# Attention and two feed-forward layers on one core: VectorE turns keys and queries, with smaller PSUM tiles and a new order of units

## The chip, the cores and the metric

The kernel runs on one core of a Trainium2 chip. The metric is the device time of one execution in microseconds (us). TensorE is called PE, VectorE DVE, ScalarE ACT, GpSimd POOL, and SyncE, which issues every DMA here, SP.

## The reference, cut to what matters

All in float32: 4 batches of 8 heads, 576 positions, 64 columns a head; then two feed-forward layers on 2304 tokens of 512 columns, with 2048 hidden columns.

```python
scores = (q @ k.T) / sqrt(64)                # per batch and head
scores = where(block_i >= block_j, scores, -1e9)   # blocks of 64 positions
attn = exp(scores - max); attn = attn / (attn.sum + 1e-9)
x = attn @ v                                 # heads side by side: 2304 x 512
x = g1(x @ w_in1) @ w_out1                   # g1: squared ramp between -1 and 1
x = (h * cos(h)) @ w_out2,  h = x @ w_in2
```

Scores need the 64 columns of a head on the partitions for both operands, so keys and queries have to be turned (positions by columns becomes columns by positions) before PE can multiply them.

## The kernel before, in words

Two heads make a pair: 16 pairs, n = 0 to 15. For each pair, `load` (L430) brings K and Q from memory as 96 partitions x 6 groups of positions, two DMAs each (one a head, 576 runs of 256 bytes). `prep` (L464) turns one of them: six PE transposes (L472) into a PSUM tile, then one copy of 128x576 to SBUF by ACT or DVE (`cp`, recorded at L185 on ACT, L189 and L190 on DVE; the copy of Q carries the scale). There are 32 preps, named "pk" (keys) and "pq" (queries). The unit's end issues the load for pair n + 2 into the buffer that it has read.

`scores` (L482) is a unit "S3", "S2" or "S0": score matmuls (L495) into a tile of two PSUM banks, maxima by DVE (L504), exponentials with row sums by ACT (L510), then `recip` (an addition, L519, and a reciprocal, L523, both DVE) and `div`, in which POOL scales P (L532). `tails` ("tl", L553) does the last 64 positions of two pairs together. `trans` ("T3", "T2", "T0", "Ta", "Tb") transposes P on PE (L590) and copies it to SBUF; `pv` ("PV", L618), `pv_halves` ("PX", L629), `pv_tails` ("Pt", L673) and `tail_halves` ("Px") multiply by V; the result goes through the tile xs to memory. P has one buffer.

PSUM has eight banks, held as four tiles of two banks. `ps_take` picks the tile that a model says is free first, or one that the unit names. A wait is for the whole tile, both banks.

`PERIOD` (L1161) is the order of units on PE for two pairs; it is laid out for all pairs in turn, with pair 1's preps put in by hand at the start. Behind the last scores and tails, the remaining units alternate with the first hidden products of layer 1 (`mm1`, L755). The opening runs idle matmuls (L702) on zeros while the first loads come.

All of this is given to `Plan` (L27), which simulates the engines P, V, A, G and S (SP) with a cost for each piece and emits every engine's instructions in simulated order. The order of units on PE is fixed by `PERIOD`; where a copy may run on two engines ("AV": ACT or DVE) the plan chooses, and it sets SP's order of DMAs too. During the pairs, 14 of the 32 weight blocks of layer 1 (512 KB each) are loaded and split (L260, L265, L277, L286, L292, L187, L181), one behind each "S3". Layer 1 then runs PE back to back (L755, L796), and layer 2 follows (L938, L1030).

Of the kernel before, what the change touches and what calls it, by code (L numbers as in the profile page):

```python
# [102 lines left out]
def attn_moe_moe_kernel(ctx: ExitStack, tc: tile.TileContext, q, k, v, w_in1, w_out1, w_in2, w_out2, out):  # L103
# [259 lines left out]
    BANKS = [0.0] * 4  # L363
    tiles, pt = {}, [0.0]

    def ps_take(cost, hold, allowed=range(4)):
        i = min(allowed, key=lambda i: (BANKS[i], i))
        start = max(pt[0], BANKS[i])
        pt[0] = start + cost
        BANKS[i] = pt[0] + hold  # L370
        n = len(tiles)
        tiles[n] = None
        return n, i, ("ps", i)

    def ps_of(n, i):
        if tiles[n] is None:
            tiles[n] = M.ps[i // 2].tile([128, 2, 512], F32, name=f"t{i}", tag=f"t{i}")
        return tiles[n]
# [6 lines left out]
    def attention_buffers(stack):  # L385
# [4 lines left out]
        M.R = [[sb.tile([TK, S // TK, 2, D], F32, name=f"r{nm}{c}") for c in range(2)] for nm in "kq"]  # L390
        M.xs = [sb.tile([128, S], F32, name=f"xs{c}") for c in range(3)]
        M.sm = sb.tile([128, 3, 3, 10], F32, name="sm")

# [20 lines left out]
    def probs(i):  # L414
        return M.A2.view(256 * P_BLOCK[i], [S if i in ("a", "b") else 64 * i + 64])
# [14 lines left out]
    def load(n, which):  # L430
# [23 lines left out]
        else:  # L454
            t = M.R[which][n % 2]
            keys = [("raw", which, n % 2)]

            def emit():
                for h in range(2):
                    nc.sync.dma_start(out=t[:, :, h, :], in_=src[b, 2 * p + h].rearrange("(t p) d -> p t d", p=TK))  # L460

        dma(294 + 64 * (which == 2), [], keys, emit)

    def prep(n, which, allowed=range(4)):  # L464
        nt = S // TK // 2
        t = M.R[which][n % 2]
        r, i, key = ps_take(0.5, 1.2, allowed)

        def emit():
            ps = ps_of(r, i)  # L470
            for j in range(2 * nt):
                pin(nc.tensor.transpose(  # L472
                    ps[:, j // nt, (j % nt) * TK:(j % nt + 1) * TK], t[:, j].rearrange("p h d -> p (h d)"),
                    ident[0:TK, 0:TK],
                ))

        tensor(0.5, [("raw", which, n % 2)], [key], emit)
        dst = (M.K, M.Q)[which][n % 2]
        cp("AV", S, lambda: dst.rearrange("p (a b) -> p a b", a=2), lambda: ps_of(r, i)[:, :, 0:HALF],
           [key], [("KQ"[which], n % 2)], scale=(1.0, scale)[which])  # L480

    def scores(n, u, allowed=range(4)):  # L482
# [3 lines left out]
        r, i_, key = ps_take(SCORES[u], {3: 3.4, 2: 3.6, 0: 3.4}[u], allowed)  # L486

        def emit():
            ps = ps_of(r, i_)
            Q, K = M.Q[c], M.K[c]  # L490
            for i, a, off in subs:
                for h in range(2):
# [3 lines left out]
                        out=ps[o:o + 64, a, off:off + 64 * i + 64], lhsT=Q[hd, 64 * i:64 * i + 64],  # L496
# [3 lines left out]
        tensor(SCORES[u], [("K", c), ("Q", c)], [key], emit)  # L500
        for i, a, off in subs:
            nk = 64 * i + 64
            do("V", 0.065 + nk / 960.0, [key], sk(0, n, i, i + 1), lambda e, i=i, a=a, off=off, nk=nk: pin(
                nc.vector.tensor_reduce(  # L504
                    out=stat(0, n, i, i + 1), in_=ps_of(r, i_)[:, a, off:off + nk], axis=AX.X, op=ALU.max, negate=True,
                )))
        for i, a, off in subs:
            nk = 64 * i + 64
            do("A", 0.24 + 0.00083 * nk, [key] + sk(0, n, subs[-1][0], subs[0][0] + 1), [("P", i)] + sk(1, n, i, i + 1),
               lambda e, i=i, a=a, off=off, nk=nk: pin(nc.scalar.activation(  # L510
                   out=probs(i)[:, 0:nk], in_=ps_of(r, i_)[:, a, off:off + nk], func=ACTF.Exp,
                   bias=stat(0, n, i, i + 1), accum_out=stat(1, n, i, i + 1),
               )))
        recip(n, subs[-1][0], subs[0][0] + 1)
        for i, a, off in subs:
            div(n, i, i)
# [9 lines left out]
    def div(n, e0, i):  # L526

        nk = S if i in ("a", "b") else 64 * i + 64
        main = nk - 64 if i in HALF_IN else nk

        def piece(out, w, writes):
            do("G", 0.25 + 0.00082 * w, sk(2, n, e0, e0 + 1) + [("P", i)], [writes], lambda e: pin(nc.gpsimd.tensor_scalar(  # L532
                out=out(), in0=probs(i)[:, 0:main] if w == main else probs(i)[:, main:nk],
# [3 lines left out]
        piece(lambda: probs(i)[:, 0:main], main, ("P", i))  # L537
        if i in HALF_IN:
            piece(lambda: M.A2.view(256 * HALF_OF[HALF_IN[i]], [64]), 64, ("PH", i))

    def tails(n, allowed=range(4)):

        both = [ps_take(0.5, 2.6 + 0.8 * x, allowed[x:][:1] if len(allowed) == 2 else allowed) for x in range(2)]

        def emit():
            ps = [ps_of(r, i) for r, i, _ in both]
            for a in range(2):
                for x in range(2):
                    for h in range(2):
# [4 lines left out]
                            out=ps[x][o:o + 64, a, 0:HALF], lhsT=M.Q[m % 2][hd, S - TAIL:S],  # L554
# [618 lines left out]
    def part_one():  # L1173
# [59 lines left out]
        for x in seq[:last + 1]:  # L1233
            unit(*x)
# [96 lines left out]
```

## Time and profile before

| | us |
|---|---|
| median of 3 runs | 928.95 (928.42 to 933.76) |
| the profiled execution's own time | 928.82 |
| its span in the trace | 927.0 |
| PE busy | 914.4 |
| DVE, ACT, POOL busy | 655.9, 562.2, 171.5 |
| the pairs' stage, from the first matmul to the first product of layer 1 that stands behind attention's last | 0.99 to 179.76 |

Busy means that an instruction of the engine is under way; a busy PE may still work below its best rate. Time outside the span (1.8 us) is the start and end of the program. Granted clock is TensorE's clock as a share of its full speed. A pass of `PERIOD` is called a period below; from 57.82 to 137.04 us four of them stand in the trace, cut where the eight transposes of a "T3" begin.

### The profile page before, as it was taken

To read this page: it belongs to the slowest core of one execution; us is meant where nothing else is said; L and a number is where in the kernel's file an instruction comes from. 1 tells how busy PE (TensorE), PEld (TensorE's weight loads), DVE (VectorE), ACT (ScalarE), POOL (GpSimd) and SP (SyncE) were. 2 spreads that over 40 slices of the span, in tenths; PEclk is the share of its full clock that TensorE was granted. 3 is DMA by queue.
4 is the path that set the end of the run, shared out by engine and by line. 5 is a ranking of instruction groups with operands and counts; after the bars stand their busy time and mean duration, and the time that the engine had idled before them with its cause. 6 is when DMAs were issued, how large, how long until landed. Compare 5 with 4: busy or idle time off the path is not lost.

```text
span 927.0 us, 18120 instructions
## 1 busy us (share of the span) xinstructions
PE 914.4 (99%) x6916; PEld 819.0 (88%) x6916; DVE 655.9 (71%) x1044; ACT 562.2 (61%) x1015; POOL 171.5 (19%) x289
## 2 busy tenths in 40 slices
PE   8999999999999999999999999999999999999998
PEld 6777777788888889988888889999999999999997
DVE  5899888768666666676226323999959899388883
ACT  5897878788666656556335434676416674166641
POOL 2667776542101112231000000000000000000000
PEclk9999999999999999999999999999999999999999
DMA  9876674584866666755120506877898878877781
GB/s 190 196 193 178 173 177 111 181 268 140 288 213 215 238 197 231 237 199 205 45 91 23 204 23 227 250 254 245 274 343 256 263 241 260 296 254 251 247 263 54
DMA packets 145670, 189.93 MB, mean 205 GB/s; under 512 B 70320, under 2 KB 103600, under 8 KB 145584
## 3 DMA queue, kind: packets, MB, share of 16 engines
q1 hardware_dynamic: 145584, 188.78, 64.6%
q8 instruction: 55, 0.90, 0.4%
q14 instruction: 31, 0.25, 0.1%
HBM read 145.23 MB, written 43.52 MB: 204 GB/s over the span
## 4 chain that ended last, share of the span: by engine, by line
PE 94%; DVE 2%; ACT 2%; POOL 1%; issue 1%; DVEq 0%; ACTq 0%; POOLq 0%
PE a L796 21%; PE h L755 21%; PE q L1030 20%; PE q L938 19%; PE t L590 4%; PE t L495 3%; PE t L618 3%; PE t L472 1%; ACT n L510 1%; DVE sm L504 1%; PE t L629 1%; PE t L702 1%; PE t L553 1%; POOL n L532 1%; PE t L673 0%
## 5 line engine op out<-in xcount | busy, mean ns | idle before, releaser
L938 PE MATMUL q<-m 128*128 128x384 f32 x1008 | 175.2, 334 | 0.0
L938 PEld LDWEIGHTS q<-m 128*128 128x128 f32 x1008 | 174.7, 188 | 0.1
L1030 PE MATMUL q<-m,n 128*128 128x256 f32 x1260 | 153.8, 283 | 0.0
L1030 PEld LDWEIGHTS q<-m,n 128*128 128x128 f32 x1260 | 152.4, 192 | 0.0
L796 PE MATMUL a<-g,m 128*128 128x512 f32 (+1 forms) x540 | 118.3, 368 | 0.6 <-DVE xs L190 0.6
L768 ACT ACTIVATE f<-h,half 128x512 f32<-128x512 f32 (+1 forms) x80 | 51.5, 644 | 103.7 <-PE h L755 103.6
L770 DVE SCALAR_TENSOR_TENSOR f<-f,h 128x512 f32<-128x512 f32 (+1 forms) x80 | 50.5, 632 | 88.9 <-ACT f L769 88.3
L796 PEld LDWEIGHTS a<-g,m 128*128 128x128 f32 x540 | 94.6, 189 | 17.5 <-ACT f L769 0.7
L532 POOL TENSOR_SCALAR n<-n,sm 128x64 f32<-128x64 f32 (+6 forms) x184 | 85.9, 488 | 44.1 <-DVE sm L523 30.2
L181 DVE TENSOR_TENSOR g<-f,g 128x512 fp32r<-128x512 f32 (+1 forms) x80 | 54.3, 679 | 37.2 <-ACT g L185 31.8
L510 ACT ACTIVATE n<-t,sm 128x384 f32<-128x384 f32 (+7 forms) x128 | 62.2, 510 | 9.1 <-DVE sm L504 4.9
L755 PE MATMUL h<-m 128*128 128x512 f32 (+1 forms) x324 | 67.5, 356 | 0.0
L755 PEld LDWEIGHTS h<-m 128*128 128x128 f32 x324 | 53.9, 189 | 8.4
L504 DVE TENSOR_REDUCE sm<-t 128x1 f32<-128x256 f32 (+7 forms) x128 | 50.0, 448 | 15.7 <-PE t L495 15.5
L185 ACT ACTIVATE g<-f 128x512 fp32r<-128x512 f32 (+1 forms) x69 | 40.4, 586 | 33.8 <-DVE f L770 33.8
L292 DVE SCALAR_TENSOR_TENSOR f<-f 128x512 uint32<-128x512 uint32 x64 | 44.7, 706 | 20.1 <-ACT f L277 17.1
L907 ACT ACTIVATE f<-f,hpi 128x768 f32<-128x768 f32 x48 | 44.6, 929 | 16.3 <-DVE f L903 16.3
L796 PE MATMUL a<-g,n 128*128 128x512 f32 (+1 forms) x240 | 52.5, 368 | 0.0
L590 PE MATMUL t<-ident,n 128*128 128x128 f32 x360 | 49.0, 277 | 3.4 <-ACT xs L185 0.9
L755 PE MATMUL h<-x,m 128*128 128x512 f32 x216 | 52.0, 389 | 0.0
L796 PEld LDWEIGHTS a<-g,n 128*128 128x128 f32 x240 | 42.1, 189 | 7.5
L769 ACT ACTIVATE f<-f 128x512 f32<-128x512 f32 (+1 forms) x80 | 46.9, 587 | 1.8
(134 smaller groups left out, 1565.3 us busy)
## 6 DMA issues: line engine op xcount, KB each, us to landing
m<-w2i SPq DMA_DIRECT2D x84, 512.0 KB, 4.4
m<-w2o SPq DMA_DIRECT2D x84, 512.0 KB, 4.2
f<-in_moe_w_in_dram SPq DMA_DIRECT2D x32, 512.0 KB, 4.5
f<-in_moe_w_out_dram SPq DMA_DIRECT2D x32, 512.0 KB, 4.4
w2i<-f SPq DMA_DIRECT2D x8, 1024.0 KB, 4.9
w2o<-f SPq DMA_DIRECT2D x8, 1024.0 KB, 4.2
w2i<-o SPq DMA_DIRECT2D x8, 768.0 KB, 3.8
w2o<-o SPq DMA_DIRECT2D x8, 768.0 KB, 4.2
```

Source lines behind the costliest of these rows:

```text
L181: return (eng or nc.vector).tensor_tensor(out=lo, in0=raw, in1=hi.bitcast(F32), op=ALU.subtract)
L504: nc.vector.tensor_reduce(out=stat(0, n, i, i + 1), in_=ps_of(r, i_)[:, a, off:off + nk], axis=AX.X, op=ALU.max, negate=True,)))
L510: lambda e, i=i, a=a, off=off, nk=nk: pin(nc.scalar.activation(out=probs(i)[:, 0:nk], in_=ps_of(r, i_)[:, a, off:off + nk], func=ACTF.Exp, ...
L532: do("G", 0.25 + 0.00082 * w, sk(2, n, e0, e0 + 1) + [("P", i)], [writes], lambda e: pin(nc.gpsimd.tensor_scalar(out=out(), in0=probs(i)[: ...
L590: pin(nc.tensor.transpose(ps[:, 128 * n:128 * (n + 1)], in_, ident))
L755: pin(nc.tensor.matmul(out=h_of(), lhsT=wt[:, a, kk * 128:(kk + 1) * 128], rhs=x[:, b, 0:w], start=(kk == 0 and i == 0), stop=(kk == NK - ...
L768: nc.scalar.activation(out=g(), in_=h_of(), func=ACTF.Relu, bias=half, scale=0.5)))
L769: do("A", 0.05 + 0.00084 * w, E, E, lambda e: pin(nc.scalar.activation(out=g(), in_=g(), func=ACTF.Square)))
L770: do("V", 0.07 + w / 960.0, [H] + E, E, lambda e: pin(nc.vector.scalar_tensor_tensor(out=g(), in0=g(), scalar=1.0, in1=h_of(), op0=ALU.min ...
L796: pin(nc.tensor.matmul(out=o, lhsT=wt[:, a, dm:dm + 128], rhs=b, start=(f == 0 and i == 0 and c == 0), stop=(f == NF - 1 and i == 2), skip ...
L938: pin(nc.tensor.matmul(out=ps[:, e, 0:HT], lhsT=w[:, e, a, 128 * kk:128 * (kk + 1)], rhs=L2.xq[i][:, kk, c], start=(not src and kk == 0 an ...
L1030: pin(nc.tensor.matmul(out=ps[:, m // 2, 256 * (m % 2):256 * (m % 2) + 256], lhsT=t[:, e, a, 128 * m:128 * (m + 1)], rhs=w[:, e, o], start ...
```

## The change

- From pair 2 on, K and Q are no longer turned by PE. `load` brings each as 32 partitions x 18 blocks for each half head, in four DMAs of 576 runs of 128 bytes; `turn` then transposes all 32x32 blocks of the 128x576 tile by one DVE instruction from SBUF to SBUF. For Q, POOL first multiplies the tile by the scale in place. These 28 turns take no PSUM and no PE. The first two pairs are prepared by PE as before.
- The loads of pair 0 come in halves, first half of K, first half of Q, second halves, and each half is turned and copied by itself ("ka", "qa", "kb", "qb"). The first unit of scores needs the first halves alone. The idle matmuls between are 11 instead of 16.
- PSUM tiles 2 and 3 become pairs of one-bank tiles, each bank with its own waits; units on them copy to SBUF in two instructions (512 and the rest, or 256 and 256). Tiles 0 and 1 stay whole.
- P gets a second buffer, used by odd pairs. The units S3 and S2 of a pair share one recip of four columns.
- The units are listed by hand with their PSUM tiles: an opening of 35 units for pairs 0 to 4, a `PERIOD` for five passes, and a closing that has layer 1's first six half products among the last units.

```diff
@@ load @@
+        elif n < PE_PAIRS:
+            c = slice(0, 2 * NTK) if part is None else slice(NTK * part, NTK * part + NTK)
...
+        else:
+            keys = [("raw", which, n % 2, a) for a in range(2)]
+            def emit():
+                for x in range(4):
+                    nc.sync.dma_start(
+                        out=M.R[which][n % 2][32 * x:32 * x + 32, 0:S].rearrange("p (a d) -> p a d", d=32),
+                        in_=src[b, 2 * p + x // 2, :, 32 * (x % 2):32 * (x % 2) + 32].rearrange("(a r) d -> r a d", r=32),
+                    )
+        kb = 358 if which == 2 else 147 if part is not None else 294 if n < PE_PAIRS else 541
+        dma(kb, [], keys, emit)
+    def turn(n, which):
+        raw = M.R[which][n % 2][:, 0:S]
+        keys = [("raw", which, n % 2, a) for a in range(2)]
+        if which == 1:
+            do("G", 0.72, keys, keys, lambda e: pin(copy(e, raw, raw, scale)))
+        do("V", 0.065 + S / 960.0, keys, [("KQ"[which], n % 2, a) for a in range(2)],
+           lambda e: pin(nc.vector.transpose(out=(M.K, M.Q)[which][n % 2], in_=raw)))
@@ scores @@
-        recip(n, subs[-1][0], subs[0][0] + 1)
-        for i, a, off in subs:
-            div(n, i, i)
+        if u == 0:
+            recip(n, 0, 4)
...
+        elif waiting.pop(n, 0):
+            recip(n, 4, 8)
...
@@ trans @@
+        if split(tile_):
+            for b in range((w + 511) // 512):
+                c0, c1 = 512 * b, min(w, 512 * b + 512)
+                cp("AV", c1 - c0, lambda c0=c0, c1=c1: pt_view(u)[:, c0:c1], lambda b=b, c0=c0, c1=c1: pb(at_, b)[:, 0:c1 - c0],
+                   [bk(at_, b)], [("PT", u, b)])
@@ part_one @@
     PERIOD = (
-        ("pq", 0, 2), ("Pt", -4, 0), ("Px", -4), ("pk", 0, 2), ("T0", -2, 0), ("T2", -2, 3),
...
+        ("pk", 0), ("PX", -3), ("Px", -4), ("S2", -1, 0), ("S3", -1, 1), ("T0", -2, 3), ("pq", 1), ("T3", -2, 2),
+        ("T2", -2, 0), ("S3", 0, 3), ("pk", 1), ("Tb", -2, 1), ("S0", 0, 2), ("S2", 0, 0), ("PV", -2, 1), ("PX", -2),
+        ("Ta", -2, 3), ("T3", -1, 0), ("T2", -1, 1), ("T0", -1, 3), ("S0", 1, 2), ("tl", 0, 0, 1), ("PV", -1, 3),
+        ("Pt", -2, 2), ("pq", 2),
     )
...
+        def prepare(n, which, tile_):
+            turn(n, which) if n >= PE_PAIRS else prep(n, which, tile_)
```

## Rows read from the trace of the kernel before

**Rows 1.** The page, parts 1 and 2: busy time, and granted clock by slice.
```profile
PE 914.4 (99%) x6916; PEld 819.0 (88%) x6916; DVE 655.9 (71%) x1044; ACT 562.2 (61%) x1015; POOL 171.5 (19%) x289
PEclk9999999999999999999999999999999999999999
```

**Rows 2.** Busy time by stretch, two periods: stretch, length, engines, clock, DMA share, GB/s.
```profile
97.23:117.14 19.91, 19.58 (x305) 15.33 (x303) 17.38 (x45) 16.76 (x49) 13.84 (x27) 1.00 0.69 178
117.14:137.04 19.90, 19.58 (x305) 15.33 (x303) 17.36 (x45) 16.76 (x49) 13.82 (x27) 1.00 0.73 184
```

**Rows 3.** Waits of PE from 20 to 140 us: total, times, longest.
```profile
PE t L590 <- DVE sm L519: 0.7, 3, 0.2
```

**Rows 4.** The same stretches, the transposes of K and Q (L472) alone: PE, PEld.
```profile
117.14:137.04 19.90, 2.80 (x24) 2.17 (x24) 1.00 0.73 184
```

**Rows 5.** Timeline of PE around two preps: start, length.
```profile
85.78 0.66 PE L472 MATMUL t<-ident,rk 96*128 96x96 f32 x6
86.28 1.04 PE L590 MATMUL t<-ident,n 128*128 128x128 f32 x8
...
92.16 0.71 PE L472 MATMUL t<-ident,rq 96*128 96x96 f32 x6
92.96 1.15 PE L673 MATMUL t<-n,rv 128*64 128x64 f32 x32
```

**Rows 6.** Groups of DVE, ACT and POOL by shape, 57.82 to 137.04 us (four periods).
```profile
L190 DVE COPY n<-t 128x640 f32<-128x640 f32 x8 | 6.6, 819 | 0.2 <-PE t L590 0.2
L190 DVE COPY K<-t 128x576 f32<-128x576 f32 x4 | 3.0, 742 | 0.0
L189 DVE TENSOR_SCALAR Q<-t 128x576 f32<-128x576 f32 x4 | 2.9, 736 | 0.0
L519 DVE TENSOR_SCALAR sm<-sm 128x2 f32<-128x2 f32 x16 | 5.3, 329 | 1.7 <-ACT n L510 1.7
L523 DVE RECIPROCAL sm<-sm 128x2 f32<-128x2 f32 x16 | 2.6, 163 | 0.4
L519 DVE TENSOR_SCALAR sm<-sm 128x4 f32<-128x4 f32 x8 | 1.2, 156 | 0.0
L190 DVE COPY xs<-t 128x64 f32<-128x64 f32 x5 | 1.0, 223 | 0.0
L185 ACT ACTIVATE Q<-t 128x576 f32<-128x576 f32 x4 | 2.6, 654 | 0.0
L185 ACT ACTIVATE K<-t 128x576 f32<-128x576 f32 x4 | 2.6, 644 | 0.0
L532 POOL TENSOR_SCALAR n<-n,sm 128x576 f32<-128x576 f32 x4 | 3.0, 746 | 0.0
```

**Rows 7.** DMA packets of the four periods, then of 6 to 8 and 8 to 10 us.
```profile
DMA packets 36029, 14.41 MB, mean 182 GB/s; under 512 B 32429, under 2 KB 34477, under 8 KB 36013
q1 hardware_dynamic: 36013, 14.20, 70.7%
...
DMA packets 1609, 0.40 MB, mean 200 GB/s; under 512 B 1609, under 2 KB 1609, under 8 KB 1609
...
DMA packets 1670, 0.42 MB, mean 208 GB/s; under 512 B 1670, under 2 KB 1670, under 8 KB 1670
```

**Rows 8.** Instructions of L460 (ns min/median/max); SP's timeline of a period, first, costliest and last.
```profile
L460 SPq DMA_DIRECT2D rk<-in_k_dram x32: 312/504/1987, 0.7 to 126.6; - x32
...
97.37 1.14 SPq L441 DMA_DIRECT2D rv<-in_v_dram  x2
...
103.73 2.16 SPq L460 DMA_DIRECT2D rq<-in_q_dram  x2
...
111.09 2.36 SPq L450 DMA_DIRECT2D rv<-in_v_dram  x2
...
116.39 0.60 SPq L445 DMA_DIRECT2D rv<-in_v_dram  x1
```

**Rows 9.** Timeline of the opening: first load, first scores, first maxima.
```profile
0.74 0.95 SPq L460 DMA_DIRECT2D rk<-in_k_dram  x2
...
7.92 2.17 PE L495 MATMUL t<-K,Q 64*64 64x256 f32 x32
```

**Rows 10.** Busy time by stretch in the opening and at the end of attention (columns as rows 2).
```profile
10.00:20.00 10.00, 7.29 (x86) 5.67 (x86) 8.05 (x25) 7.04 (x23) 5.41 (x13) 1.00 0.84 175
...
160.00:180.00 20.00, 18.09 (x212) 14.60 (x207) 14.57 (x28) 15.42 (x33) 13.62 (x19) 1.00 0.50 157
180.00:200.00 20.00, 20.00 (x89) 16.53 (x89) 12.63 (x20) 15.38 (x27) 4.76 (x6) 1.00 0.81 268
```

More of the change, by code (lines that the diff above doesn't have):

```diff
@@ L361, in w_combine, with ps_take, split, pb @@
         store(3, 4, many, mk)
[L363 to L378, printed above, removed]
+    tiles = []
+    def ps_take(i):
+        tiles.append({})
+        return len(tiles) - 1, i
+    def split(i):
+        return i > 1
+    def pb(at_, b):
+        n, i = at_
+        if split(i):
+            if b not in tiles[n]:
+                tiles[n][b] = M.ps[1].tile([128, 512], F32, name=f"t{i}{b}", tag=f"t{i}{b}")
+            return tiles[n][b]
+        return whole(at_)[:, b]
+    def whole(at_):
+        n, i = at_
+        if 0 not in tiles[n]:
+            tiles[n][0] = M.ps[0].tile([128, 2, 512], F32, name=f"t{i}", tag=f"t{i}")
+        return tiles[n][0]
+    def bk(at_, b):
+        return ("ps", at_[1], b if split(at_[1]) else 0)
+    def bks(at_):
+        return [("ps", at_[1], b) for b in range(2 if split(at_[1]) else 1)]
     pairs = [(b, p) for b in range(B) for p in range(NP)]
@@ L453, in emit @@
                     )
[L454 to L456 removed]
+        elif n < PE_PAIRS:
+            c = slice(0, 2 * NTK) if part is None else slice(NTK * part, NTK * part + NTK)
+            keys = [("raw", which, n % 2, a) for a in range(2) if part in (None, a)]
             def emit():
                 for h in range(2):
[L460 removed]
@@ L469, in emit, with prep @@
+    def prep(n, which, tile_, part=None):
+        js = range(2 * NTK) if part is None else range(NTK * part, NTK * part + NTK)
+        t = raw_view(n, which)
+        cost = 0.083 * len(js)
+        at_ = ps_take(tile_)
         def emit():
-            ps = ps_of(r, i)
-            for j in range(2 * nt):
+            for j in js:
                 pin(nc.tensor.transpose(
-                    ps[:, j // nt, (j % nt) * TK:(j % nt + 1) * TK], t[:, j].rearrange("p h d -> p (h d)"),
-                    ident[0:TK, 0:TK],
-                ))
@@ L482, in scores @@
-    def scores(n, u, allowed=range(4)):
+        if part is None and not split(tile_):
+            cp("AV", S, lambda: dst.rearrange("p (a b) -> p a b", a=2), lambda: whole(at_)[:, :, 0:HALF],
+               [bk(at_, 0)], [("KQ"[which], n % 2, a) for a in halves_], scale=(1.0, scale)[which])
+            return
+        for a in halves_:
+            cp("AV", HALF, lambda a=a: dst[:, HALF * a:HALF * (a + 1)], lambda a=a: pb(at_, a - halves_[0])[:, 0:HALF],
+               [bk(at_, a - halves_[0])], [("KQ"[which], n % 2, a)], scale=(1.0, scale)[which])
@@ L1181, in part_one @@
         M.z = z.bitcast(BF16)
-        r, i, _ = ps_take(4.0, 0.0)
-        idle(36, ps_of(r, i))
+        idle(36, pb(ps_take(0), 0))
         consts()
+        for part in range(2):
+            for which in range(2):
+                load(0, which, part)
+        for which in range(2):
+            load(1, which)
         for n in range(2):
-            for which in range(2):
-                load(n, which)
             load(n, 2)
```

277 lines of the change are left out of this document (153 added, 124 removed), and 16 rows, old and new, of tables (CLOSING, OPENING, PERIOD).

## The prediction

> **What bounds the kernel now.** I read the page's busy shares first. PE is busy for 914.4 of 927.0 us and no other engine comes near [rows 1]; the granted clock is full in all slices, so nothing here is a clock effect. The change touches only the pairs' stage, so next I read the stretches. Two periods of 19.9 us stand there [rows 2]: PE busy 19.58, DVE 17.4, ACT 16.8, POOL 13.8. Then the waits of PE: between 20 and 140 us it is kept waiting for 0.7 us in all [rows 3]. So PE's own instructions set the period, and DVE and ACT have 2.5 and 3.1 us of room. Behind the stage PE runs without a gap (20.00 of 20.00 from 180 us, [rows 10]), and that part is not edited, so what the stage gains or loses reaches the end unchanged.
>
> **The change part by part.** I count per period (two pairs) and multiply by 7, because pairs 2 to 15 are moved.
>
> *PE transposes removed.* A period has four preps, 24 transposes, and PE is busy in them for 2.80 us [rows 4]. From start to start, the step that PE really needs, one prep takes 0.50 us (85.78 to 86.28) where transposes follow and 0.80 us (92.16 to 92.96) where the kind of matmul changes [rows 5]. Four times 0.50 is 2.0, the lower bound; 2.8 is the upper. I take 2.4, the middle, since part of the change-over stays with the unit that follows. PE then needs 19.9 - 2.4 = 17.5 us.
>
> *Copies removed, DVE transposes added.* Four copies of 128x576 a period go: two on DVE at 0.74 us, two on ACT at 0.65 us [rows 6], so 1.5 and 1.3 us. Four DVE transposes of 128x576 come. The trace has none. The nearest row is DVE's copy of the same shape, 0.742 us; I take that: 3.0 us. The upper bound is twice it, 5.9 us, if a transpose walks its data twice; the lower is 1.5 us, if reading SBUF instead of PSUM doubles the rate.
>
> *Recips merged.* A period had four two-column recips (0.329 + 0.163 us) in excess; two four-column ones (0.156 + about 0.163) replace them [rows 6]: 2.0 - 0.6 = 1.3 us off DVE. Part of the 0.329 is waiting, so this may be as little as 0.6.
>
> *Split copies.* Four units of the new period lie on split tiles and copy twice where they copied once (T0 twice, T3, PV). What a copy costs beside its width comes from 0.223 us at 64 columns and 0.819 at 640 on DVE [rows 6]: 1.035 ns a column, and 0.157 us that stays. Four of them: 0.6 us, on DVE or ACT.
>
> DVE and ACT together: 17.4 + 16.8 - 1.5 - 1.3 + 3.0 - 1.3 + 0.6 = 33.7 us, 16.9 each, as the plan may put the copies of P and xs on either. POOL gets two scalings of 128x576 at 0.746 us [rows 6]: 13.8 + 1.5 = 15.3 us. A wait comes with it: POOL multiplies Q, then DVE turns it. Queued behind the turn on DVE are maxima and copies, which PE waits for through its tiles. The turn is due about a period after its load, so the plan can place it late enough; I cost the wait at nothing. If that cover fails, one POOL scaling (0.75 us) a pair is exposed, 1.5 a period.
>
> *Loads.* Before: 36,029 packets in four periods, 9,007 a period; under 512 bytes, 8,107 [rows 7]. Keys and queries are 4 x 1,152 = 4,608 of 256 bytes; they become 9,216 of 128 bytes. What a packet costs when the engines are full is read from the opening: 1,609 and 1,670 packets in 2 us each on 16 engines, 19.9 and 19.2 ns a packet of 256 bytes [rows 7]. The bounds for one of 128 bytes are half that, 9.8, and the same, 19.6. DMA time is 70.7% of 19.8 us = 14.0 us a period; the change adds between 0 and 4,608 x 19.6 ns / 16 = 5.6 us. I take the middle, 2.8: 16.8 us.
>
> [...] No run here shows a packet of 128 bytes yet.
>
> *SP.* In the period from 97.37 SP issues 24 DMAs in 15 lines that add up to 15.0 us, the first 1.14 and the last 0.60 [rows 8]. Eight DMAs are added. An issue of a K or Q load takes 0.50 us in the median, 0.31 at least, and 1.08 where the queue pushes back (2.16 for two) [rows 8]. So 15.0 + 8 x 0.50 = 19.0 us, between 17.5 and 23.6. But of the 15.0 some 2.2 us are push-back (2.16 and 2.36 where such pairs of issues otherwise take about 1.05 and 1.30), and the plan may let weight loads fall behind keys and queries. So SP needs 16.8 to 19.0. I read it as nearly full and not yet the bound.
>
> *What sets the new period.* PE needs 17.5, DVE and ACT 16.9 each, SP and DMA about 17 to 19. Five resources so close don't interleave without gaps. Before, DVE kept 2.5 us free; I let the new bound be PE with 1.0 us of waiting: 18.5 us (17.5 to 19.3). Gain 19.9 - 18.5 = 1.4 us a period, 7 x 1.4 = 9.8.
>
> *Opening.* The first scores start at 7.92 us though K's load is issued from 0.74 [rows 9]: two whole loads have to land and be turned before them, in the new opening only two halves. From 10 to 20 us PE is idle for 2.7 us [rows 10]. I take 1.5 us of gain, between -1 (more issues on SP ahead of pair 1's loads) and 3.
>
> *P's second buffer, one-bank tiles, the closing.* They take waits away, and PE has nearly none in the period; their worth is already in the 18.5. From 160 to 180 PE is idle for 1.9 us [rows 10]; of that I take 0.7 (between -1 and 1.5).
>
> **Sum.** 9.8 + 1.5 + 0.7 = 12.0 us off the profiled execution's own 928.82 us (927.0 of span and 1.8 around it), which is 0.1 under the median of the runs: 916.8, say 917. The likeliest case's own range is 909 to 922.
>
> **The rivals.**
> 1. *SP becomes the bound.* The median issue and today's push-back give 19.0 us a period; with gaps 19.4. For it: 15.0 of 19.9 us are already issuing. Against it: a K or Q load is asked for two pairs ahead, and 1 MB of weights a period can wait. Gain 0.5 x 7 + 1.5 = 5: 924.
> 2. *Small packets fill the DMA engines: slower than before.* If a packet of 128 bytes costs what one of 256 does, DMA time is 14.0 + 5.6 = 19.6 us a period in packets alone, and the highest share over a whole period here is 73% [rows 2]. At 90% of full engines the period is 21.8, that is 1.9 longer, 13 in seven; less 1.5 of the opening: 940. It decides from about 16 ns a packet of 128 bytes: then 14.0 + (9,216 x 16 - 4,608 x 19.6) ns / 16 = 17.6, over 0.9 is 19.5 us, and next to nothing of the gain is left. For it: in the opening the engines move 200 GB/s when full, and behind the stage, in bigger packets, 268 at a share of only 0.81 [rows 7, 10]. Against it: weights can be put off past the pairs.
> 3. *DVE's transposes cost twice a copy.* 33.7 + 3.0 = 36.7, so DVE and ACT need 18.4 each, with the same 1.0 of waiting 19.4. Gain 0.5 x 7 + 1.5 = 5, as in rival 1, but with SP idle: 924.
> 4. *The chain stays.* PE's work is shorter, but score, maximum, exponential, POOL's division, transpose and product of one pair follow each other as before, and PE waits for them: the removed 2.4 us turn into idle PE, and only the opening's 1.5 is left: 927. The second P buffer and the two pairs in flight speak against it.
>
> [...]
>
> **How the numbers follow.** Forecast 0.56; rival 1, 0.16; rival 2, 0.15; rival 3, 0.07; rival 4, 0.06. The range that leaves no more than 2 in 10 out takes in the forecast's better side and rivals 1, 3 and 4 whole, and the nearer part of rival 2: 906 to 934. One per cent, 9.3 us, is about what a measurement of this kernel can tell from no change. Under 919.7: most of the forecast and little of rival 1, 0.54. Over 938.2: the far half of rival 2, 0.10. The rest, 0.36, is within.
>
> **What would show it.** Right: a period of 18 to 19 us with PE idle for about 1 us in it, DVE's transpose rows near 0.74 us, no L472 behind pair 1, 32 DMAs a period with SP free for some of the time, and attention's end near 168 us. Wrong: SP's or the DMA engines' share near full with turns that wait for loads (rivals 1 and 2), a DVE transpose of 1.2 us or more (rival 3), PE idle for 2 us a period behind POOL or ACT (rival 4).

## The result, and the profile after

The changed kernel takes 934.58 us (median of 20 runs, 930.26 to 937.71) against 928.69 for the kernel before on the same chips: a ratio of 1.0055 [1.0042, 1.0069]. It is 5.9 us slower; the forecast was 917, 11.7 faster, in a range that ended at 934. The profiled execution was the slowest of its 20 (937.71 us, span 935.6), so the losses read from it are the larger ones.

The page of the kernel after, parts 1 to 3, to be set beside [rows 1]:

```profile
PE 907.3 (97%) x6738; PEld 808.5 (86%) x6738; DVE 661.4 (71%) x1043; ACT 555.0 (59%) x1027; POOL 177.6 (19%) x302
...
PEclk9989999999989999999999999999999999999999
...
DMA packets 178886, 189.91 MB, mean 203 GB/s; under 512 B 103537, under 2 KB 136817, under 8 KB 178801
```

PE is busy for 7.1 us less in a span 8.6 us longer, and its clock, full throughout before, dips in two slices: at about 47 us, in the pairs' stage, and at about 270, in layer 1. Two losses, then. Behind the pairs' stage, layer 1's first product starts at 182.38 us instead of 179.76, so 2.6 us are lost there (36 matmuls of layer 1 stand ahead of it in both kernels); the other 6.0 are lost later.

The stretches of four periods, the answer to [rows 2] (same columns; cut where the four transposes of the unit behind a "PX" begin):

```profile
51.81:69.47 17.66, 17.27 (x279) 13.27 (x279) 16.12 (x43) 12.98 (x40) 12.99 (x26) 1.00 0.65 134
69.47:90.00 20.53, 18.04 (x281) 13.39 (x281) 17.12 (x44) 12.68 (x43) 12.29 (x26) 1.00 0.63 127
90.00:110.64 20.64, 18.88 (x277) 13.75 (x276) 16.42 (x41) 14.09 (x48) 12.83 (x26) 0.92 0.75 148
110.64:133.57 22.93, 19.11 (x278) 14.71 (x279) 17.07 (x44) 14.44 (x51) 13.90 (x28) 0.93 0.69 135
```

The first shows what the new order can do: 17.66 us, PE busy for 17.27. The other three take 20.5 to 22.9, and no engine is full in them. The mean is 20.4, where it was 19.9. The waits of PE from 20 to 300 us, against [rows 3]:

```profile
PE t L689 <- DMA rv<-in_v_dram: 8.5, 5, 5.6
PE t L654 <- POOL n L597: 3.6, 5, 1.4
PE t L689 <- ACT n L567: 3.3, 1, 3.3
PE a L872 <- DVE o L190: 3.1, 1, 3.1
```

The largest names a load that the change does not touch: the values (rv), which PE needs for P times V. (The third, at 128.76 us, is put down to ACT, but stands at the same instruction and is followed by a wait for rv; it may be a late value load as well, which is not shown.) SP's timeline ahead of the longest of these waits says why (start, length of the issues, line, what, how many DMAs):

```profile
29.65 3.67 SPq L497 DMA_DIRECT2D rq<-in_q_dram  x3
33.37 0.74 SPq L260 DMA_DIRECT2D f<-in_moe_w_in_dram  x1
34.16 0.98 SPq L265 DMA_DIRECT2D f<-in_moe_w_out_dram  x2
35.23 3.11 SPq L497 DMA_DIRECT2D rk<-in_k_dram  x4
38.44 1.76 SPq L731 DMA_DIRECT2D x1d<-xs  x1
40.30 2.04 SPq L478 DMA_DIRECT2D rv<-in_v_dram  x2
42.43 1.62 SPq L497 DMA_DIRECT2D rq<-in_q_dram  x3
44.16 1.35 SPq L469 DMA_DIRECT2D rv<-in_v_dram  x2
45.61 0.62 SPq L478 DMA_DIRECT2D rv<-in_v_dram  x1
```

Each line begins where the one before it ends, with nothing waited for: SP issues without a break. The two large value DMAs (L469) are issued at 44.16 and PE starts on them at 46.93; they are late because they were issued late, behind keys and queries of later pairs. From 60 to 140 us SP's timeline adds up to 120 DMAs and 75.65 of 80 us, 0.63 us each; before, it was 97 DMAs and 58.32 of 79.22 us, 0.60 each. A single issue of a key or query DMA still takes 0.50 us in the median (L497), as in [rows 8]; the rest is push-back: issues that stand longer in SP, up to 2.6 us for one.

The idle PE pays twice here. PE's timeline around the same wait, and the next unit of the same kind:

```profile
39.86 1.42 PE L551 MATMUL t<-K,Q 64*64 64x256 f32 x24
46.93 4.39 PE L689 MATMUL t<-n,rv 128*64 128x128 f32 x40 [5.64 <-DMA rv<-in_v_dram]
...
56.08 2.00 PE L689 MATMUL t<-n,rv 128*64 128x128 f32 x40
```

Busy time in stretches of 2 us over the same place (clock is the third column from the right):

```profile
42.00:44.00 2.00, 0.00 (x0) 0.00 (x0) 1.69 (x5) 1.56 (x7) 1.92 (x4) 1.00 0.34 68
44.00:46.00 2.00, 0.00 (x0) 0.00 (x0) 0.00 (x0) 1.11 (x7) 0.00 (x0) 0.67 0.72 131
46.00:48.00 2.00, 1.01 (x6) 0.64 (x8) 0.00 (x0) 0.00 (x0) 0.00 (x0) 0.50 0.52 118
48.00:50.00 2.00, 2.00 (x25) 2.00 (x23) 0.00 (x0) 0.00 (x0) 0.00 (x0) 0.50 0.64 146
50.00:52.00 2.00, 2.00 (x35) 1.82 (x32) 0.11 (x1) 0.00 (x0) 0.08 (x1) 0.62 0.57 99
52.00:54.00 2.00, 2.00 (x21) 2.00 (x20) 1.97 (x6) 0.69 (x1) 1.49 (x3) 1.00 0.85 163
```

Behind 5.6 us of idle PE the granted clock is 0.50 (46 to 50 us), and 40 matmuls that take 2.00 us at 56.08, where it is 1.00, take 4.39 (PE's weight loads wait another 0.46 us for rv in them). So this one late load costs 5.6 + 2.4 us.

The second of PE's waits, for POOL's divisions (n), has late loads behind it too, for 2.9 of its 3.6 us. POOL scales each Q tile when it has landed, and the next divisions stand behind that in its order. POOL's largest wait from 20 to 180 us (total, times, longest), and one place where PE feels it, in POOL's timeline and then in PE's:

```profile
POOL rq L187 <- DMA rq<-in_q_dram: 32.1, 9, 8.0
...
98.14 0.67 POOL L187 TENSOR_SCALAR rq<-rq 128x576 f32<-128x576 f32 x1 [3.98 <-DMA rq<-in_q_dram]
...
100.44 1.13 PE L654 MATMUL t<-ident,n 128*128 128x128 f32 x4 [1.38 <-POOL n L597]
```

PE waits another 0.25 us in the same unit. It is the same at 78.55 and 79.62 us: POOL waits 4.20 us for a query load, and PE then 0.99 and 0.25 for n.

The second loss stands in layer 1, which the diff does not edit. PE's timeline there:

```profile
266.73 2.88 PE L831 MATMUL h<-x,m 128*128 128x512 f32 x12
269.45 1.52 PE L872 MATMUL a<-g,m 128*128 128x512 f32 x6
274.09 2.93 PE L872 MATMUL a<-g,m 128*128 128x512 f32 x6 [3.13 <-DVE o L190]
276.82 4.50 PE L831 MATMUL h<-x,m 128*128 128x512 f32 x12
```

And the timeline of SP and DVE there, those that touch the tile o and the weights:

```profile
265.57 1.58 SPq L260 DMA_DIRECT2D f<-in_moe_w_in_dram  x2
...
267.37 1.92 SPq L885 DMA_DIRECT2D x2d<-o  x4
...
273.35 0.69 DVE L190 COPY o<-a 128x512 f32<-128x512 f32 x1 [0.86 <-DMA x2d<-o]
```

The store of o lands late, with two weight loads of 512 KB issued just ahead of it. DVE is at other work until 272.49 us and then waits 0.86 us more for that store before it can copy the next result into o; the PSUM tile stays taken, and PE idles for 3.13 us and then runs 12 matmuls in 4.50 us instead of 2.88 (the granted clock is 0.50 from 274 to 280 us). Attention had issued fewer of them: 2 from 51.8 to 133.6 us, where it had been 8 in 79 us. Whether that is why, e6, e13 and e14 below test.

What the change meant to do is there. The turns are one DVE instruction each (groups of DVE by shape, 51.81 to 133.57 us; for [rows 6]):

```profile
L511 DVE STREAM_TRANSPOSE Q<-rq 128x576 f32<-128x576 f32 x8 | 6.1, 764 | 0.0
L511 DVE STREAM_TRANSPOSE K<-rk 128x576 f32<-128x576 f32 x8 | 6.0, 753 | 0.0
```

The first scores start at 6.95 us instead of 7.92 [rows 9], and from 10 to 20 us PE is busy for 8.86 instead of 7.29 [rows 10].

### The profile page after: what moved, and what is told of

It is laid out like the page before. It is cut to its first block, busy times and chain, and to the rows that moved or that the text cites. A ratio compares the mean times of both kernels' runs of the same rounds, so it can differ in the third digit from the quotient of the medians.

```text
span 935.6 us, 17845 instructions
## 1 busy us (share of the span) xinstructions
PE 907.3 (97%) x6738; PEld 808.5 (86%) x6738; DVE 661.4 (71%) x1043; ACT 555.0 (59%) x1027; POOL 177.6 (19%) x302
## 4 chain that ended last, share of the span: by engine, by line
PE 88%; DMA 5%; DVE 2%; SPq 2%; ACT 1%; issue 1%; POOL 0%; POOLq 0%; DVEq 0%; ACTq 0%
PE a L872 20%; PE h L831 20%; PE q L1106 19%; PE q L1014 19%; PE t L689 3%; PE t L654 3%; PE t L551 2%; DMA rv<-in_v_dram 2%; SPq L497 1%; DMA rk<-in_k_dram 1%; DVE sm L560 1%; DMA m<-x1d 1%; PE t L617 1%; DMA x2d<-o 1%; PE t L700 1%
## 5 line engine op out<-in xcount | busy, mean ns | idle before, releaser
L872 PEld LDWEIGHTS a<-g,m 128*128 128x128 f32 x540 | 95.4, 190 | 20.5 <-DVE o L190 3.5
L560 DVE TENSOR_REDUCE sm<-t 128x1 f32<-128x128 f32 (+7 forms) x128 | 49.8, 446 | 12.1 <-PE t L551 11.4
L292 DVE SCALAR_TENSOR_TENSOR f<-f 128x512 uint32<-128x512 uint32 x64 | 46.6, 736 | 13.8 <-ACT f L277 10.4
L185 ACT ACTIVATE g<-f 128x512 fp32r<-128x512 f32 (+1 forms) x62 | 36.7, 592 | 29.4 <-DVE f L846 29.2
L597 POOL TENSOR_SCALAR n<-n,sm 128x64 f32<-128x64 f32 (+6 forms) x104 | 51.2, 510 | 6.7 <-DVE sm L587 4.0
L689 PEld LDWEIGHTS t<-n,rv 128*64 128x64 f32 x640 | 33.8, 147 | 21.4 <-issue 9.2
L831 PEld LDWEIGHTS h<-x,m 128*128 128x128 f32 x216 | 41.7, 194 | 8.8
L689 PE MATMUL t<-n,rv 128*64 128x128 f32 (+1 forms) x640 | 37.3, 269 | 12.1 <-DMA rv<-in_v_dram 8.5
```

The lines of the kernel that those rows point to most:

```text
L292: pin(nc.vector.scalar_tensor_tensor(out=v().bitcast(U32), in0=t.bitcast(U32), scalar=3, in1=w.bitcast(U32), op0=ALU.logical_shift_left, o ...
L560: nc.vector.tensor_reduce(out=stat(0, n, i, i + 1), in_=pb(at_, a)[:, off:off + nk], axis=AX.X, op=ALU.max, negate=True,)))
L597: do("G", 0.25 + 0.00082 * w, sk(2, n, e0, e0 + 1) + [P_(i, n)], [writes], lambda e: pin(nc.gpsimd.tensor_scalar(out=out(), in0=probs(i, m ...
L689: pin(nc.tensor.matmul(out=out_.rearrange("p (e b) -> p e b", b=64) if j < x else out_, lhsT=V[:, j, h, :], rhs=rhs if j < x else rhs[:, 0 ...
L831: pin(nc.tensor.matmul(out=h_of(), lhsT=wt[:, a, kk * 128:(kk + 1) * 128], rhs=x[:, b, 0:w], start=(kk == 0 and i == 0), stop=(kk == NK - ...
L872: pin(nc.tensor.matmul(out=o, lhsT=wt[:, a, dm:dm + 128], rhs=b, start=(f == 0 and i == 0 and c == 0), stop=(f == NF - 1 and i == 2), skip ...
```

## The experiments

Two theories. **The queue:** SP issues one DMA after another, four instead of two for a load make it the bound, and what it issues late (values) stops PE. **The small runs:** runs of 128 bytes hold the 16 DMA engines up, whoever issues them. In the table, SP is the sum of its issues from 60 to 140 us, and "end" is the start of layer 1's first product behind attention.

| run | median us | ratio to before | SP, us of 80 (DMAs) | end, us |
|---|---|---|---|---|
| before | 928.69 | 1 | 58.32 of 79.22 (97) | 179.76 |
| after | 934.58 | 1.0055 [1.0042, 1.0069] | 75.65 (120) | 182.38 |
| e1 before, four DMAs of 128-byte runs | 942.83 | 1.0137 [1.0102, 1.0173] | 74.53 (122) | 193.16 |
| e2 before, four DMAs of 256-byte runs | 938.17 | 1.0084 [1.0055, 1.0112] | 74.44 (124) | 189.15 |
| e3 after, half the runs | 922.72 | 0.9932 [0.9909, 0.9955] | 74.07 (129) | 171.35 |
| e4 after, half the DMAs | 910.28 | 0.9793 [0.9752, 0.9834] | 60.01 (100) | 158.59 |
| e5 keys on ACT | 930.43 | 1.0017 [0.9998, 1.0035] | 54.77 (85) | 182.41 |
| e6 weights not put off | 939.49 | 1.0121 [1.0106, 1.0137] | 73.49 (119) | 188.48 |
| e7 small value loads on ACT | 934.52 | 1.0067 [1.0049, 1.0084] | 53.08 (94) | 181.29 |
| e8 the same, planned | 931.92 | 1.0034 [1.0023, 1.0046] | 59.2 (103) | 181.25 |
| e9 keys on POOL | 926.7 | 0.9969 [0.995, 0.9988] | 57.96 (98) | 175.98 |
| e10 e4 with keys on ACT | 914.66 | 0.9848 [0.9822, 0.9873] | 50.07 (83) | 162.82 |
| e11 only keys turned | 925.66 | 0.9967 [0.9956, 0.9979] | 72.43 (117) | 176.18 |
| e12 half the key DMAs on POOL | 923.24 | 0.9938 [0.9921, 0.9955] | 72.62 (115) | 169.66 |
| e13 e12, key weights earlier | 926.38 | 0.9977 [0.9958, 0.9997] | 70.74 (114) | 175.78 |
| e14 e12, weights not put off | 937.24 | 1.0086 [1.006, 1.0113] | 70.46 (109) | 185.59 |

**e1 and e2: the loads alone, on the kernel before.** The load of pairs 2 to 15 is cut in four, by columns (e1) or by positions (e2):

```diff
-                    nc.sync.dma_start(out=t[:, :, h, :], in_=src[b, 2 * p + h].rearrange("(t p) d -> p t d", p=TK))
@@ e1 @@
+                    w = 64 if n < 2 else 32
+                    for c in range(0, 64, w):
+                        nc.sync.dma_start(
+                            out=t[:, :, h, c:c + w], in_=src[b, 2 * p + h, :, c:c + w].rearrange("(t p) d -> p t d", p=TK))
@@ e2 @@
+                    w = 6 if n < 2 else 3
+                    for c in range(0, 6, w):
+                        nc.sync.dma_start(
+                            out=t[:, c:c + w, h, :], in_=src[b, 2 * p + h].rearrange("(t p) d -> p t d", p=TK)[:, c:c + w])
```

> The kernel before, whose K and Q loads from pair 2 on are issued as in the changed kernel: four DMAs of 576 runs of 128 bytes instead of two of 576 runs of 256. All the rest, PE transposes included, stays. If the loads alone explain the loss: SP needs 14.6 us a period in issues now (58.3 in four), 8 more at 0.50 make 18.6, and with about 0.09 between issues 21.5 in place of 19.85, so some 1.6 us in each of six to seven periods: 937 to 941 us. If the DVE turns, the split tiles or the order of units are the cause: 929 us, as before.

> The kernel before with four DMAs for each K and Q load from pair 2 on, each 288 runs of 256 bytes: more issues, but the same packets as before. SP theory (the number of issues counts): the same as with the small runs, 937 to 941 us. Packet theory (the number of packets counts): no change, 929 us.

The number of DMAs alone, same runs and same bytes, costs 9.2 us (938.17 against 928.93 beside it), as the SP theory had it, and PE waits for rv, 5.3 us in e2 and 9.3 in e1, in a kernel that never had that wait. The shorter runs cost 4.7 more; with them e1 is 1.8 above its range. The DMA queue of both from 60 to 140 us (packets, MB, share of 16 engines), e1 and then e2; last, that of the kernel before from 6 to 8 us, which the prediction took for full engines [rows 7]:

```profile
q1 hardware_dynamic: 51201, 13.26, 76.3%
```

```profile
q1 hardware_dynamic: 35536, 13.53, 66.2%
```

```profile
q1 hardware_dynamic: 1609, 0.40, 136.8%
```

Both stayed far below the share of the opening; the share adds up the times of packets, and at 136.8% some of them must overlap. SP issued for 74.5 us of 80 in both. The shorter runs lengthen the median issue of a query DMA from 456 to 506 ns, so they too reach the time by way of SP at least in part.

**e3 and e4: half of it taken away, on the kernel after.** e3 keeps the four DMAs and loads half the positions in each; e4 keeps the length and issues two of the four.

```diff
@@ e3 @@
-                        out=M.R[which][n % 2][32 * x:32 * x + 32, 0:S].rearrange("p (a d) -> p a d", d=32),
-                        in_=src[b, 2 * p + x // 2, :, 32 * (x % 2):32 * (x % 2) + 32].rearrange("(a r) d -> r a d", r=32),
+                        out=M.R[which][n % 2][32 * x:32 * x + 32, 0:HALF].rearrange("p (a d) -> p a d", d=32),
+                        in_=src[b, 2 * p + x // 2, 0:HALF, 32 * (x % 2):32 * (x % 2) + 32].rearrange("(a r) d -> r a d", r=32),
@@ e4 @@
-                for x in range(4):
+                for x in range(2):
```

> The changed kernel with the same four DMAs for each turned K and Q, each of half the runs (positions 0 to 287 alone are loaded; the other half of the tile keeps what it had, so scores there use old keys and queries). Packets of K and Q are back to 4,608 a period, the number of DMAs is unchanged. SP theory: at most 2 us off the changed kernel's 934.6, as push-back goes: 932 to 935. Packet theory: the period falls to about 18.5 us, 917 to 921.

> The changed kernel with two instead of four DMAs for each turned K and Q, of whole length (only the first head of the pair is loaded; the partitions of the second keep what they had). Packets as in the run with half the runs, DMAs as in the kernel before. SP theory: SP has room again, PE waits for no load, the period is about 18.3 us and the granted clock stays full: 915 to 921. Packet theory: the same time as with half the runs and four DMAs. If PE, DVE and ACT were the bound all along: 930 or more here too.

Half the packets and half the bytes of K and Q at the same count of DMAs (e3) give 11.9 us. The SP theory had expected 2 at most and missed; the time lies 1.7 above the packet theory's range. SP stays as full, but an issue takes 0.574 us instead of 0.63, so more of them go through in the same 80 us (129, not 120). Half the DMAs at the same packets and bytes (e4) give 12.4 more, 4.7 below the SP theory's range: from 60 to 140 us both move about as many (36,960 and 35,661), and e4 is the one in which SP has room. The small-runs theory has no reason for the second step; the queue theory has one for both, though not the size of the first. e4's stretches of 60 to 80 and 80 to 100 us:

```profile
60.00:80.00 20.00, 19.94 (x321) 15.82 (x315) 19.54 (x48) 15.97 (x57) 14.37 (x30) 1.00 0.52 111
80.00:100.00 20.00, 19.94 (x341) 15.45 (x335) 19.51 (x54) 15.48 (x56) 16.19 (x35) 1.00 0.57 134
```

PE full, DVE nearly so, the clock at 1.00, no wait for rv left: this is the rest of the change without the loads in its way. Four periods of it take 47.47 to 115.15 us, 16.9 each.

**e5, e7, e8: SP relieved by ACT.** e5 has ACT issue the key DMAs, e7 the three small value DMAs of a pair, and e8 gives e7's issues to the planner as work of ACT.

```diff
@@ e5, the loads of four DMAs @@
-                    nc.sync.dma_start(
+                    (nc.sync if which else nc.scalar).dma_start(
@@ e7 and e8, the small value loads @@
-                nc.sync.dma_start(
+                nc.scalar.dma_start(
```

> The changed kernel, complete, with the DMAs of the turned K issued by ACT and not by SP; same DMAs, same packets, the same order otherwise. Theory that SP's issuing is the bound: SP has 24 DMAs a period as in the kernel before, so it has room as in the run with half the issues; packets are full, so somewhat behind that run's 910: 913 to 922 us. Theory that the DMA engines are full: no change, 932 to 937. A third price: ACT gets 8 issues of 0.50 us, 4 us a period on 13.6 busy; if it becomes the bound, 924 to 930.

> The changed kernel with the three small DMAs of each V load (64 partitions, 32 KB, 0.60 us an issue) issued by ACT: six DMAs a period off SP, 3.6 us. SP theory: 26 DMAs at 0.57 to 0.63 make 15 to 16.4 us a period: 914 to 923. DMA engines full: 932 to 937. ACT as a new bound: 3.6 us on 13.6, less than with the keys, so at most 925.

> As with the small V loads on ACT, and the plan knows it: 1.9 us of ACT for three of them, SP's V load counted at 256 KB. The order of units on PE is the same. 912 to 921 if SP's issuing is the bound; a version meant to beat both kernels. 925 or more if ACT's issues land in front of the exponentials that PE waits for.

All three gave SP back what the queue theory asks for (53 to 59 us of 80) and won 4 us at most; its ranges failed. e5 is 0.4 above the range of its third price, e8 in its second range, and e7 in that of full DMA engines. But the engines' share is not the reason in e7 (60.9 and 4.6% on its two queues from 60 to 140 us). PE's waits for rv are gone in all three, and waits put down to ACT stand in their place: from 20 to 300 us, for P 10.6 us in e7 and 9.5 in e8. ACT's timeline in e5 shows how; then PE's:

```profile
90.20 0.38 ACT L567 ACTIVATE n<-t,sm 128x128 f32<-128x128 f32 x1
90.45 0.22 ACT L567 ACTIVATION_READ_ACCUMULATOR n<-t,sm 128x1 f32 x1
91.47 1.59 ACTq L497 DMA_DIRECT2D rk<-in_k_dram  x2
93.11 0.31 ACT L567 ACTIVATE n<-t,sm 128x64 f32<-128x64 f32 x1 [2.44 <-DMA rq<-in_q_dram]
```

```profile
93.56 1.35 PE L551 MATMUL t<-K,Q 64*64 64x256 f32 x16 [2.74 <-ACT n L567]
```

The last small exponential of a unit stands behind two issues of key DMAs in ACT's order. For 2.44 us ACT executes nothing (the two issues take 1.59 of it), and PE waits 2.74 us for that exponential. (The DMA of queries named there is inferred from the event that came last; the exponential does not read it.) What e5 saved was SP's time to issue (54.77 us of 80 instead of 75.65); queries and values landed later (3.3 and 4.1 us in the median, against 2.5 and 2.9 in the kernel after).

**e9, e12: SP relieved by POOL.** All four key DMAs of a load on POOL (e9), or every second one (e12).

```diff
-                    nc.sync.dma_start(
@@ e9 @@
+                    (nc.sync if which else nc.gpsimd).dma_start(
@@ e12 @@
+                    (nc.sync if which or x % 2 else nc.gpsimd).dma_start(
```

> The kernel after with the four DMAs of each key load of the third pair on issued by GpSimd instead of SyncE: the same DMAs, the same 128-byte runs, nothing left out; SP is left with 85 DMAs between 60 and 140 us instead of 120, as with ScalarE's queue (930.43 us). Theory A (SP's queue alone was the bound, and ScalarE's queue gave nothing back because an issue on ScalarE stands in front of the exponentials and copies for which TensorE waits): GpSimd is busy only 12 of 20 us there, so the waits for rv go and little comes in their place, 912 to 922. Theory B (the loads with 128-byte runs land late however they are issued, since the queues share the 16 DMA engines): keys land later than 3 us and the time stays at 928 to 938. Theory C (GpSimd's own issue is dear, and the divisions behind it reach TensorE late): 935 to 950, with TensorE waiting for the divisions n and the query's scaling rq.

> The kernel after with two of the four DMAs of each key load of the third pair on issued by GpSimd, the other two by SyncE as in the kernel after; nothing is left out. With all four on GpSimd (926.7 us) one issue took 0.67 us of GpSimd and it was full (19.8 of 20 us), while SP had 22 us of 80 over. Split, GpSimd has 4 issues a period, 2.7 us on top of some 14 of 20, and SP about 28 DMAs a period, as where only the keys are turned (72 of 80 us). Theory A (the time is set by whichever issuing engine is full, and neither is here): 915 to 922, with no wait of TensorE for rv or for n above 3 us in all. Theory B (the 128-byte runs themselves land late by sharing the DMA engines): 925 to 932, landings of 3.5 us and more, TensorE waiting whatever the queues.

e9 lies between its theories A and B. PE's waits for rv are gone, but an issue is 0.67 us of work for POOL, which is then full, and PE's largest wait is for POOL's n, 8.2 us from 20 to 300 us: the sign of theory C, without its time (groups of POOL, and its stretch, 60 to 140 us and 100 to 120 us, of e9):

```profile
L497 POOL DMA_DIRECT2D rk<-in_k_dram x32 | 21.4, 674 | 0.0
```

```profile
100.00:120.00 20.00, 19.25 (x299) 14.20 (x296) 19.48 (x55) 14.12 (x48) 19.77 (x40) 1.00 0.87 164
```

Split over both (e12), neither is full, and it is 923.24 us: 5.4 under the kernel before and 11 under the kernel after, the best of all that do the whole work. It missed its window of 915 to 922 by 1.2, and the waits for n, 5.0 us, its bound of 3. Both runs change one thing more than the issuing engine. The profile counts other packets on POOL's queue, here e9's from 60 to 140 us (packets, MB, share):

```profile
q0 software_dynamic: 1552, 2.37, 14.9%
```

That is about 1.5 KB a packet for the same 128-byte runs. The engines' share did not fall by it (72.6% on both queues in e9 and 74.4% in e12, against 67.4% in the kernel after), but e12's gain can't be laid to SP's relief alone. Its landings are long (issues of e12 from 60 to 140 us, median from issue to landing last):

```profile
rv<-in_v_dram SPq DMA_DIRECT2D x19, 128.0 KB, 4.0
...
rq<-in_q_dram SPq DMA_DIRECT2D x29, 72.0 KB, 4.1
...
rk<-in_k_dram SPq DMA_DIRECT2D x16, 72.0 KB, 2.6
rk<-in_k_dram POOLq DMA_DIRECT2D x15, 72.0 KB, 4.2
```

In the kernel after the same loads landed in 2.9, 2.5 and 2.7 us, and it was slower. So longer landings did not by themselves make a kernel slower. e12's waits for rv are 0.6 us in all, which fits the queue theory, where it counts when a DMA is issued.

**e10: the price of ACT's issues by itself.** e4 with its key DMAs on ACT, where SP had room already.

> The kernel with two whole-length DMAs per load (910.28 us, second head's keys and queries left out as there), with the key DMAs issued by ScalarE. SP's queue already had room there (60 of 80 us), so nothing is to be gained and the price of an issue on ScalarE shows by itself: about 4 key DMAs a period at 0.32 us. If ScalarE's order is what ate the gain (theory A), 913 to 920, and TensorE waits for exponentials or copies. If it was the landing of the small runs (theory B), ScalarE had 4 us of 20 to spare and the time stays at 909 to 912.

It lost 4.4 us, in theory A's range: ACT's issues cost of themselves. The profiled executions took 917.22 us (e10) and 909.09 (e4), 8.1 apart: 4.2 at attention's end (162.82 against 158.59) and the rest behind it, where PE waits 3.7 us for o. PE's waits name ACT for only part of it, so how the issues cost this is not shown.

**e11: fewer DMAs.** VectorE turns the keys, PE the queries as before, in two DMAs.

```diff
@@ load, the planner's figure, the lists of units @@
...
@@ prepare @@
-            turn(n, which) if n >= PE_PAIRS else prep(n, which, tile_)
+            turn(n, which) if n >= PE_PAIRS and which == 0 else prep(n, which, tile_)
```

> The kernel after with VectorE turning the keys alone: queries are loaded as in the kernel before (two DMAs with 256-byte runs) and turned by TensorE into a PSUM tile, the unit order changed for the four places where that needs a tile. Nothing is left out. DMAs of a period go from 32 to 28, GpSimd loses the scaling of the queries (2 x 0.67 us), VectorE one of two turns (2 x 0.76 us) and with ScalarE gains the copies out of PSUM (2 x 0.7 us), TensorE gains 2 x 0.5 us and its switches. If the number of DMAs on SP's queue sets the time, 28 x 0.58 = 16.2 us of issue fit into a period of 18.5 us and it comes to 915 to 922, ahead of both kernels. If the new stalls (PSUM tiles shared with the query, TensorE at 18.6 us) replace the old, 924 to 932.

925.66: 3.0 us better than before, in the second of its ranges and not in the 915 to 922 of the first. PE is busy for 19.2 of 20 us from 60 to 140 us, no single wait is over 3 us and none is for rv: PE's own work, with the query's transposes back in it, is nearly the whole of the time again.

**e6, e13, e14: the second loss.** The planner books a key or query load at 541 KB instead of 294, and so lets weight loads fall behind. e6 books 294 in the kernel after; e13 and e14 do so in e12, for the keys or for both.

```diff
-        kb = 358 if which == 2 else 147 if part is not None else 294 if n < PE_PAIRS else 541
@@ e6, e14 @@
+        kb = 358 if which == 2 else 147 if part is not None else 294
@@ e13 @@
+        kb = 358 if which == 2 else 147 if part is not None else 294 if n < PE_PAIRS or which == 0 else 541
```

> The changed kernel where the plan counts a turned K or Q load as 294 KB in place of 541, as for the old loads: the same instructions in another order, weight loads earlier among the pairs. SP theory: SP is full in either order; more weight loads ahead of K, Q and V move attention's end later by 1 to 4 us, and the wait of PE near 270 us (3.1 us, and the low clock behind it) shrinks: 930 to 938. If the plan's price is what costs the time: under 925.

> The kernel of the run before (two of four key DMAs on GpSimd, 923.24 us) with the planner's figure for a key load of the third pair on set to the 294 of the kernel before, not 541, since SyncE now issues only two of the four; the planner then puts off fewer weight conversions from attention into layer 1. Nothing else changes. Theory D (the second loss, the one idle stretch of TensorE at some 270 us where an a-product waits 3.1 us for o, comes from weights put off): the stretch shrinks to under 1.5 us and the time comes to 917 to 922. Theory E (SP's queue has no room for those weights in attention: 72.6 of 80 us issuing): attention gets longer by as much or more, 923 to 930.

> The same with 294 for key and query loads alike, so that the planner spaces the weights as the kernel before did. On the kernel after itself this figure made it slower by 5 us (939.49 us). Theory D: the idle stretch at 270 us is gone altogether and the time is 917 to 922, as in the run beside it or below it. Theory E: SP runs late in attention again, waits for rv of over 2 us come back, and it is 925 to 934.

PE's wait for o in layer 1, 3.1 us in the kernel after and in e12, is 1.2 in e6, 0.3 in e13 and 1.2 in e14. So it hangs on the weights put off, though not step by step. But attention ends 6 us later in e6 and in e13, and 16 later in e14: the weights cost more there than they save behind it. The times (e6 1.5 above the SP theory's range, e13 in theory E's, e14 3.2 above it) go that way, but theory E's sign did not come: in e13 and e14 no wait for rv is left, and PE waits 8.4 and 10.5 us for POOL's n, where it was 5.0 in e12. In e14 POOL itself waits 20.8 us for query loads, 11.8 in e12 (20 to 180 us). The higher figure, with which the second loss comes, is the better choice of the two.

## Why the prediction was wrong

- **What failed: "So SP needs 16.8 to 19.0. I read it as nearly full and not yet the bound."** SP's term was made of 15.0 us, plus 8 issues at the median of 0.50, less 2.2 of push-back that was to go away. Measured, a DMA took 0.63 us of SP in the mean, push-back included, and 120 of them in 80 us make 19.3 us of a period of 20.4. The 15.0 of [rows 8] were already 0.625 for each of 24 DMAs: the same price for 32 would have given 20.0. The median hid the long issues, and push-back did not go away with more DMAs.
- **A queue was counted like an engine.** The 1.0 us of waiting was to cover all five resources. But SP issued one DMA behind the other, and what came late was the one load that PE needs next. Where SP issued for 74 of 80 us or more (after, e1, e2, e3), PE waited for rv for 5 to 9 us; at 73.5 (e6) for 1.2, at 72.6 (e12) for 0.6.
- **"I cost the wait at nothing", of POOL's scaling, failed as well.** The cover was that a turn is due long after its load. In the kernel after POOL waited 32.1 us for nine late query loads, and 2.9 of the 3.6 us that PE waited for its divisions stand right behind two of these; in e4, where SP had room, POOL waited once, 4.5 us, and PE 0.2 for n.
- **"What the stage gains or loses reaches the end unchanged" failed.** 2.6 us were lost at the end of the stage and 6.0 more in layer 1, which no edit touched: the planner moved weight loads there.
- **Rival 1 had the mechanism, not the price.** It gave 19.4 us a period and 924; the period is 20.4. "1 MB of weights a period can wait" was its counter-argument, and they did wait (2 loads in four periods, not 8): the queue was full all the same, and the waiting weights made the second loss, some 6 us in the profiled run, which no rival held.
- **The clock was left out.** "So nothing here is a clock effect" held for the kernel before, where PE hardly idled. In the kernel after a late load of 5.6 us cost 8.0.
- **Small packets, rival 2: fell.** Its condition was 16 ns for a packet of 128 bytes. From e1 and e2, 0.101 of 16 engines x 80 us for 15,665 packets more is 8.3 ns for each packet that became two; the estimate of 9.7 (2.8 us a period) was near. In e5, whose keys have ACT's queue to themselves, 18,078 packets took 20.6% of the same, 14.6 ns each, somewhat under the condition. The share stayed at 67% in the kernel after, and the 90% that rival 2 took for full engines was no bound: it was 136.8% in the opening. The runs did cost time, 4.7 us on the old kernel, at a share of 76.3%.
- **DVE's turns, 0.742 us: right.** 0.753 for keys and 0.764 for queries, where DVE's copy of the same shape took 0.742 [rows 6]; rival 3 fell.
- **PE's saving and the new order: right, and with room to spare.** PE was to need 17.5 us; the best period of the kernel after takes 17.66, and with the loads out of the way (e4) a period takes 16.9 and the time is 910.28. PE is busy there for 896.9 us, 17.5 less than before, where the forecast had 7 x 2.4 = 16.8. The gain of e4 is 18.6 us (against 928.93 beside it) where the sum had 12.0. It is an upper figure, since e4 leaves half of the keys and queries unloaded. Rival 4 fell with it.
- **Opening, 1.5 us: borne out as far as the rows go,** by the first scores (1.0 earlier) and PE's 1.6 us more from 10 to 20 us; no run has the opening alone. The closing's 0.7 can't be read from these runs, as weights shift across it.

Left open: how much of the shorter runs' cost is SP's longer issue and how much the DMA engines, and how much of e12's gain POOL's larger packets made. And e12 is still 13 us behind e4; its waits name n (5.0 us), P (1.8) and o (3.1). Of those for n, 2.3 us come where two key issues of 1.36 us stand on POOL ahead of a division (18.71 us), and 2.7 behind a query load for which POOL stood still for 7.2 us (until 33.97); no run took the rest apart.

## What to carry to other kernels

Count DMAs as instructions of the engine that issues them, at the mean with push-back and not at the median (0.63 and 0.50 us on SP in the kernel after). Here a queue that issued for 74 of 80 us or more kept PE waiting for a load, and what it delays need not be what was added to it. Before splitting a load, ask which engine has room for the issue itself: an engine whose next instructions PE waits for has less than its busy share shows, as ACT had in e5 and POOL in e9 (in the kernel after they were busy for 51.8 and 46.8 of 80 us). And look at the clock behind each wait of PE: behind those of 3.1 and 5.6 us in the kernel after it was 0.50, and they cost more than their length.

## What the runs showed of the hardware

- The issue of one DMA took 0.32 us on ACT in the median (e5), 0.50 in the median on SP (the kernel after) and 0.67 in the mean on POOL (e9), for the same 576 runs of 128 bytes; only on POOL does it show as busy time.
- With the keys, or half of them, on a second queue, loads left on SP's landed later: the 128 KB value loads in 4.0 us (e9, e12) and 4.1 (e5) instead of 2.9, the queries in 3.0 (e9) to 4.1 (e12) instead of 2.5; the keys left on SP in e12 did not (2.6 instead of 2.7). All three kernels were faster than the one after.
- From 128-byte runs, POOL's queue made 1,552 packets for 32 key DMAs of 72 KB (e9), as the profile counts them; on ACT's queue there are 18,078 packets for 28 such DMAs (e5).
- The share of the DMA engines' queue passed 100%: 136.8% from 6 to 8 us of the kernel before.
- Behind a PE idle for 5.6 us the granted clock was 0.50 from 46 to 50 us and 1.00 again from 52, with PE busy from 46.93 on.
